# Attention into two mixture stages on one core: first-batch scores of two heads issued in turn on both row halves, second-batch sinks on all rows, new durations for the planner

## The chip, the cores and the metric

The kernel runs on one core of a Trainium2 chip. The metric is the device time of one execution in microseconds; lower is better. The time of the kernel before is the median of three runs.

## The reference

Sliding-window attention with sink positions, then two dense stages on its output (token-major, 1536 x 512), all in float32:

```
scores = q @ k.T / 8; keep = (key < n_sink) | (0 <= query - key < window)     # batch 2, 8 heads, 768, 64
a = exp(where(keep, scores, -1e9) - max); a = a / (sum(a) + 1e-9); x = a @ v   # n_sink 4, window 128
out1 = sum_e p[:, e] * (relu(x @ w1[e]) @ w2[e])     # 4 experts, 512 -> 1024 -> 512, p = normalised domain_probs
out  = ((out1 @ w_a) * (out1 @ w_b)) @ w_out         # 512 -> 1536 -> 512
```

## The kernel before, in words

Each float32 factor is split into a high and a low part, and a product is the sum of three TensorE products (high x high, high x low, low x high).

**Attention.** A unit is one batch b, one block m of 256 queries (3 per batch) and one pair of heads hp (4): 12 units per batch. `scores` makes, for each of the two heads h and two query tiles qi, a product of 128 queries by up to 288 keys (a previous block, 32 sink columns, the own block) into one PSUM bank; VectorE adds the penalty and takes the minimum as it reads the bank, ScalarE takes the exponential with its sum, and after the second tile of a head VectorE adds epsilon to both sums, takes reciprocals, and `nc.either` scales the weights on GpSimd, ScalarE or VectorE. `values` transposes the weights of the unit before, splits them (tile pt), multiplies them by the values (vv), and for m > 0 adds the sink part from sq, sk and the sink values vs.

The head size is 64, half of TensorE's 128 rows. In the first batch a head's queries and keys lie on its own 64 partitions (0 to 63 or 64 to 127), and a score product is three half-row matrix products, qh x kh, qh x kl, ql x kh (`factors`, first form); its sinks are two full-row products for both heads together. In the second batch high and low keys are stacked on all 128 partitions (two full-row products per score product), while the sink of one head is one half-row product on that head's 64 partitions, `vsink[own, hp, 0, :], sk[own]`. In the trace the score products are bank<-kk,qh and bank<-kk,ql, the sinks bank<-sk,vs, the weighted values bank<-pt,vv, transposes bank<-ident,...

**The stages.** First the 12 units of batch 0 run, with two plain experts for batch 0 (tiles xh, uh, dh) from the second block on; then the other experts of batch 0 by a seven-product scheme (tiles th, uh, dh) with the 12 units of batch 1 beside them; then batch 1's experts and the gated stage (tiles yt), with the conversion of the gate weights beside.

**Order.** The three parts between `nc.start()` and `nc.run()` are planned. Instructions are noted as nodes in program order; successive TensorE instructions into the same bank are one node (`note`). `cost` gives each a duration, `run` works out due times backward from TensorE's program order, and places nodes by readiness and due time on the engines V, S, G, T and the DMA queue D (SyncE's), TensorE at most 8 nodes ahead. Where a node has several ways (`either`, `copied`, `combined`), the plan chooses the engine. What runs on the chip is the resulting order for each engine, with semaphores. In the first part the score banks are two ("s" is (0, 1)), in the second one.

Every instruction recorded by the planner carries line 355 in the profile, the call in `run`; so tiles tell them apart.

Of the kernel before, what the change touches and what calls it, by code (L numbers as in the profile page):

```python
# [1 line left out]

# [16 lines left out]
P = 128  # L19
SC = 32  # L20
# [7 lines left out]
def f32(ap):  # L28
    return ap.bitcast(F32)
# [65 lines left out]
class Plan:  # L95
# [22 lines left out]
    def either(self, *ways):  # L118
# [4 lines left out]
        else:  # L123
            self.note(ways)

    def start(self):
        self.nodes, self.seen, self.at, self.key, self.last = [], {}, 0.0, None, None

    @staticmethod
# [18 lines left out]
    @staticmethod  # L148
    def cost(engine, name, args, kw):

        size = 1
        for d in kw.get("out", args[0] if args else None).shape[1:]:
            size *= d
        psum = any("PSUM" in str(getattr(v, "space", "")) for v in (*args[1:], *(v for k, v in kw.items() if k != "out")))
        if engine == "T":
            return 3 + size / 2.4 * (2 if name == "transpose" else 1)
        if engine == "V":
            fast = name in ("tensor_copy", "tensor_scalar") and not psum
            return 65 + size * (0.52 if fast else 1.04) + (55 if fast and hasattr(kw.get("scalar1"), "ap") else 0)
        if engine == "S":  # L160
            return (50 if psum else 95) + size / 1.2 + (180 if "accum_out" in kw else 0)
        return {"G": 150 + size * 2.1, "D": 60 + size * 1.42}[engine]

    @staticmethod
# [12 lines left out]
    def note(self, ways):  # L177
        engine, name, call, args, kw = ways[0]
        outs = [kw[k] for k in ("out", "accum_out") if kw.get(k) is not None]
        ins = [v for k, v in kw.items() if k not in ("out", "accum_out")]  # L180
        rest = list(args)
        if not outs:
            outs.append(rest.pop(0))
        ins = [v for v in ins + rest if hasattr(v, "ap") or hasattr(v, "tensor")]
        places = [self.region(v) for v in outs]
        node = None
        if engine == "T":
            key = places[0][0], self.turn.get(places[0][0])
            node = self.last if self.key == key else None
        if engine != "T" and self.key and any(self.region(v)[0] == self.key[0] for v in (*ins, *outs)):  # L190
            self.key = None
        if node is None:
            node = {"deps": set(), "n": len(self.nodes), "at": self.at, "ways": {w[0]: [0.0, [], False] for w in ways}}
            self.nodes.append(node)
            if engine == "T":
                self.key, self.last = key, node
        for e, name, call, args, kw in ways:
            way = node["ways"][e]
            way[0] += self.cost(e, name, args, kw)
            way[1].append((call, args, kw))  # L200
            way[2] = way[2] or self.shares(e, name, args, kw)
        node["e"], node["cost"] = engine, node["ways"][engine][0]
        if engine == "T":
            self.at = node["at"] + node["cost"]
        for v in ins:
            self.touch(node, self.region(v), False)
        for r in places:
            self.touch(node, r, True)
# [152 lines left out]
def tile_kernel(ctx, tc, a0, a1, vs, limit, places, dp, w1, w2, wa, wb, wo, out):  # L361
# [105 lines left out]
    def split(hi, lo, src, psum=False):  # L467
        copied(hi, src)
        if psum:
            nc.vector.tensor_tensor(out=lo, in0=src, in1=f32(hi), op=sub)  # L470
        else:
            combined(lo, src, f32(hi), sub)
# [103 lines left out]
    def sink_values(ab, b):  # L576

        raw = ab.tile([P, HP, D], F32, tag="tmp", name="vsr")
        nc.sync.dma_start(out=raw, in_=vs[b])
        if b:  # L580
            v = ab.tile([P, HP, 1, 2 * D], F32R, tag="vs", name="vs", bufs=1)
            held["vs", b] = v
            split(v[:, :, 0, 0:D], v[:, :, 0, D:], raw)
            return
        v = ab.tile([P, HP, 2, 2 * D], F32R, tag="vs", name="vs", bufs=1)
        held["vs", b] = v

        nc.gpsimd.memset(f32(v), 0.0)
        for h in range(2):
            r, c = slice(64 * h, 64 * h + 64), slice(64 * h, 64 * h + 64)  # L590
            nc.scalar.activation(out=v[r, :, 0, c], in_=raw[r], func=copy)
            r = slice(64 * h, 64 * h + 32)
            nc.vector.tensor_tensor(out=v[r, :, 1, c], in0=raw[r], in1=f32(v[r, :, 0, c]), op=sub)

    def scores(pools, raw, u):
# [20 lines left out]
        if b == 0:  # L616
# [6 lines left out]
            def factors(h, q, k):  # L623
                hs = slice(64 * h, 64 * h + 64)
                return [(x[hs, q], kk[hs, y, k]) for x, y in ((qh, 0), (qh, 1), (ql, 0))]
# [16 lines left out]
        st = ab.tile([P, 2, 4], F32, tag="st", name="st")  # L642
        sq = ab.tile([P, 2, 2, 2, SC], F32, tag="sq", name="sq") if m else None
        u.update(vv=vv, pp=pp, sq=sq)
        for h in range(2):
            for qi in range(2):
                c = 2 * h + qi
                k0 = qi * (P + SC)
                ks, use = (slice(k0, k0 + WIN), slice(0, WIN)) if m or qi else (slice(c0, c0 + 256), cur)
                sp = bank([P, ks.stop - ks.start], "s")  # L650
                parts = factors(h, slice(qi * P, (qi + 1) * P), ks)
                for n, (lhs, rhs) in enumerate(parts):
                    nc.tensor.matmul(out=sp, lhsT=lhs, rhs=rhs, start=n == 0, stop=n == len(parts) - 1)
                seen, least = pp[:, h, qi, use], low[:, slot, c:c + 1]
                nc.vector.tensor_tensor_reduce(
                    out=seen, in0=sp[:, 0:use.stop - use.start], in1=pen[:, min(2 * m + qi, 2), use],
                    scale=-1.0 / 8.0, scalar=3e38, op0=add, op1=ALU.min, accum_out=least,
                )
                nc.scalar.activation(
                    out=seen, in_=seen, func=ACTF.Exp, scale=-1.0, bias=least, accum_out=st[:, h, qi:qi + 1],  # L660
                )
                if c == 0:
                    combined(parts_[1], vr, f32(parts_[0]), sub)
                if qi == 0:
                    yield
            rs = st[:, h, 2:4]
            nc.vector.tensor_scalar(out=rs, in0=st[:, h, 0:2], scalar1=EPS, scalar2=None, op0=add)
            nc.vector.reciprocal(out=rs, in_=rs)
            if m:
                combined(  # L670
                    sq[:, :, h], pp[:, h, :, P:P + SC].unsqueeze(2).to_broadcast([P, 2, 2, SC]),
                    rs.unsqueeze(2).unsqueeze(3).to_broadcast([P, 2, 2, SC]), ALU.mult,
                )
            for q0, cols in ((0, slice(0, WIN)),) if m else ((0, cur), (1, prev)):
                seen, r = pp[:, h, q0:, cols], rs[:, q0:]
                n = seen.shape[1]
                nc.either(
                    ("gpsimd", "tensor_tensor", dict(
                        out=seen, in0=seen, in1=r.unsqueeze(2).to_broadcast(list(seen.shape)), op=ALU.mult
                    )),  # L680
                    *(("scalar", "activation", dict(
                        out=seen[:, i], in_=seen[:, i], func=copy, scale=r[:, i:i + 1]
                    )) for i in range(n)),
                    *(("vector", "tensor_scalar", dict(
                        out=seen[:, i], in0=seen[:, i], scalar1=r[:, i:i + 1], scalar2=None, op0=ALU.mult
                    )) for i in range(n)),
                )
            yield
        yield

    def values(pools, u, x):
# [31 lines left out]
        def weighted(h):  # L723
            own, oth = slice(64 * h, 64 * h + 64), slice(64 - 64 * h, 128 - 64 * h)
            sk = made.get("sk")
            if b == 0:

                if h == 0:
                    made["o"] = bank([P, 256], "o")
                op, mm = made["o"], []  # L730
                for j, s0 in blocks:
                    mm += [
                        (vv[:, j, 3 * a + h:3 * a + h + 2].rearrange("p a d -> p (a d)"), part(h, s0, o))
                        for a, o in ((0, 0), (0, 5), (1, 0))
                    ]
                if m > 0 and h:
                    mm += [(vsink[:, hp, a, :], sk) for a in range(2)]
                first, last = h == 0, h == 1
            else:

                op, mm = bank([P, 256], "o"), []
                for j, s0 in blocks:
                    mm += [(vv[:, j, 2 * h:2 * h + 2].rearrange("p a d -> p (a d)"), part(h, s0, o)) for o in (0, 5)]
                if m > 0:
                    mm.append((vsink[own, hp, 0, :], sk[own]))
                first = last = True
            for n, (lhs, rhs) in enumerate(mm):
                nc.tensor.matmul(
# [872 lines left out]
```

## Time and profile before

| | before |
|---|---|
| median of 3 runs (lowest, highest) | 952.56 us (951.9, 953.61) |
| profiled execution: its own time, its span | 951.72 us, 949.6 us |
| mean granted TensorE clock | 0.988 |
| busy share TensorE, VectorE, ScalarE, GpSimd | 97%, 78%, 43%, 34% |
| TensorE instructions | 4845 |
| HBM read, written | 131.10 MB, 83.36 MB |

The busy time of TensorE is that of overlapping instructions: a product's listed duration holds the way through the array, and the next starts before it ends. Starts tell how fast they follow each other. A share of a stage is read from a table of stretches, not from the whole span. Starts and stretches are given in us from the span's start.

### The profile page before, as it was taken

The page shows a single profiled execution, that of the slowest core. Times are in us where ns is not written, and L with a number is a line of the kernel's source. Part 1 is how long each engine was busy: PE and PEld are TensorE (multiplying, and loading weights), DVE is VectorE, ACT ScalarE, POOL GpSimd, SP SyncE. Part 2 cuts the span into 40 slices and gives each one's busy share as a digit, 9 for nine tenths or more (in the row PEclk, how much of TensorE's full clock was granted, in tenths as well). Part 3 has the DMA queues.
Part 4 walks back from the last instruction along what each step waited for, and adds up shares of the span by engine and source line. Part 5 has one row for each costly group of instructions (what it writes and reads, how often), then busy time and mean ns, then how long its engine had stood idle before and what let it go on. Part 6 is the DMA issues. An engine that isn't in the chain of part 4 may idle for free.

```text
span 949.6 us, 13937 instructions
## 1 busy us (share of the span) xinstructions
PE 920.8 (97%) x4845; PEld 824.8 (87%) x4845; DVE 741.1 (78%) x1516; ACT 404.3 (43%) x946; POOL 324.2 (34%) x328
## 2 busy tenths in 40 slices
PE   7999989999999999999999999999999999999996
PEld 6778878898888888888989989999887789999995
DVE  6798789999999998997876878799898985333343
ACT  6677557766656573521222312143453453211111
POOL 3565445646544651520200110044254543110100
PEclk9699999999999999999999999999999999999998
DMA  4250068886566744587867777877778878755552
GB/s 150 93 204 25 2 211 319 289 289 233 181 232 239 287 170 154 202 314 253 304 225 284 248 263 245 289 252 250 272 257 296 285 287 314 268 199 199 201 198 93
DMA packets 84752, 215.47 MB, mean 227 GB/s; under 512 B 7872, under 2 KB 42176, under 8 KB 84672
## 3 DMA queue, kind: packets, MB, share of 16 engines
q1 hardware_dynamic: 84672, 214.49, 64.6%
q8 instruction: 40, 0.66, 0.3%
q14 instruction: 40, 0.33, 0.1%
HBM read 131.10 MB, written 83.36 MB: 226 GB/s over the span
## 4 chain that ended last, share of the span: by engine, by line
PE 77%; DVE 13%; DMA 5%; ACT 2%; issue 2%; POOL 1%; SPq 1%; DVEq 0%; ACTq 0%; POOLq 0%
PE bank L355 77%; DVE tu L355 2%; DMA rawu<-gu 2%; DVE ul L355 2%; DVE y L355 1%; DVE kk L355 1%; DVE c L355 1%; DVE pp L355 1%; DVE sums L355 1%; DVE hl L355 1%; DMA rawu<-in_w 1%; DVE st L355 1%; DMA scr<-in_dp 1%; DMA araw<-in_a 1%; SPq L355 1%
## 5 line engine op out<-in xcount | busy, mean ns | idle before, releaser
L355 PE MATMUL bank<-dh,hh 128*128 128x512 f32 x528 | 210.2, 398 | 0.0
L355 PE MATMUL bank<-dl,hh 128*128 128x512 f32 x528 | 208.5, 395 | 0.0
L355 PE MATMUL bank<-dh,hl 128*128 128x512 f32 x528 | 208.0, 394 | 0.0
L355 PE MATMUL bank<-xh,uh 128*128 128x384 f32 (+1 forms) x384 | 129.7, 338 | 0.7 <-DVE r L355 0.7
L355 PE MATMUL bank<-xl,uh 128*128 128x384 f32 (+1 forms) x384 | 127.2, 331 | 0.0
L355 PE MATMUL bank<-xh,ul 128*128 128x384 f32 (+1 forms) x384 | 127.1, 331 | 0.0
L355 PEld LDWEIGHTS bank<-dl,hh 128*128 128x128 f32 x528 | 99.0, 187 | 21.7
L355 PE MATMUL bank<-th,uh 128*128 128x384 f32 x324 | 109.7, 339 | 3.9 <-DVE c L355 2.5
L355 PEld LDWEIGHTS bank<-dh,hh 128*128 128x128 f32 x528 | 99.2, 188 | 13.9 <-issue 0.3
L355 PEld LDWEIGHTS bank<-dh,hl 128*128 128x128 f32 x528 | 99.2, 188 | 12.6
L355 PE MATMUL bank<-tl,uh 128*128 128x384 f32 x324 | 109.2, 337 | 0.1
L355 PE MATMUL bank<-th,ul 128*128 128x384 f32 x324 | 108.8, 336 | 0.0
L355 ACT ACTIVATE r<-bank 128x384 f32<-128x384 f32 x73 | 35.8, 491 | 146.5 <-PE bank L355 145.9
L355 ACT ACTIVATE hh<-c 128x384 fp32r<-128x384 f32 x98 | 50.8, 519 | 96.7 <-DVE c L355 95.5
L355 DVE TENSOR_TENSOR c<-bank,r 128x384 f32<-128x384 f32 x108 | 59.8, 554 | 35.1 <-PE bank L355 34.5
L355 DVE SCALAR_TENSOR_TENSOR y<-bank,prob,y 128x512 f32<-128x512 f32 x108 | 80.0, 744 | 7.3 <-PE bank L355 6.6
L355 DVE TENSOR_TENSOR c<-bank,u 128x384 f32<-128x384 f32 x54 | 29.9, 553 | 67.6 <-PE bank L355 64.4
L355 PEld LDWEIGHTS bank<-xh,uh 128*128 128x128 f32 x384 | 72.7, 189 | 7.3 <-issue 1.1
L355 PEld LDWEIGHTS bank<-xl,uh 128*128 128x128 f32 x384 | 72.8, 190 | 4.4
L355 PEld LDWEIGHTS bank<-xh,ul 128*128 128x128 f32 x384 | 72.7, 189 | 0.0
L355 PEld LDWEIGHTS bank<-th,uh 128*128 128x128 f32 x324 | 60.8, 188 | 9.1 <-DVE c L355 3.7
L355 POOL TENSOR_TENSOR ul<-sums,uh 128x256 fp32r<-128x256 f32 (+1 forms) x39 | 40.6, 1043 | 80.7 <-ACT uh L355 80.6
(147 smaller groups left out, 1860.5 us busy)
## 6 DMA issues: line engine op xcount, KB each, us to landing
ue<-uh SPq DMA_DIRECT2D x14, 896.0 KB, 4.3
ue<-ul SPq DMA_DIRECT2D x14, 896.0 KB, 6.1
uh<-ue SPq DMA_DIRECT2D x14, 896.0 KB, 4.8
ul<-ue SPq DMA_DIRECT2D x14, 896.0 KB, 6.8
ug<-uh SPq DMA_DIRECT2D x12, 896.0 KB, 5.4
ug<-ul SPq DMA_DIRECT2D x12, 896.0 KB, 7.8
uh<-ug SPq DMA_DIRECT2D x12, 896.0 KB, 4.7
ul<-ug SPq DMA_DIRECT2D x12, 896.0 KB, 6.8
```

What stands on the lines that cost most here:

```text
L355: call(*args, **kw)
```

## The change

Four things change. In the first batch, `product` issues a query tile's products for both heads in turn (head 0, head 1, three times) into two banks, as one node of the plan, held together by `nc.together()`; both heads' sums and reciprocals are then one instruction each. In the second batch the sink values get a second, zero half, so that each head's sink is a product on all rows. The second batch's scores keep the order by heads. The planner's durations of TensorE instructions and of scaled copies on ScalarE change.

```diff
+    @contextmanager
+    def together(self):
+        self.hold, self.key = True, None
+        yield
+        self.hold, self.key = False, None
...
-            return 3 + size / 2.4 * (2 if name == "transpose" else 1)
+            half = "lhsT" in kw and kw["lhsT"].shape[0] < P
+            return 1 + size * (0.84 if name == "transpose" else 0.35 if half else 0.4535)
...
-            return (50 if psum else 95) + size / 1.2 + (180 if "accum_out" in kw else 0)
+            return (50 if psum else 95) + size / 1.2 + (180 if "accum_out" in kw else 0) + (
+                85 if hasattr(kw.get("scale"), "ap") else 0)
...
-            node = self.last if self.key == key else None
+            node = self.last if self.key == key or self.hold and self.key else None
...
-            v = ab.tile([P, HP, 1, 2 * D], F32R, tag="vs", name="vs", bufs=1)
+            v = ab.tile([P, HP, 2, 2 * D], F32R, tag="vs", name="vs", bufs=1)
             held["vs", b] = v
-            split(v[:, :, 0, 0:D], v[:, :, 0, D:], raw)
+            nc.gpsimd.memset(f32(v), 0.0)
+            for h in range(2):
+                r = slice(64 * h, 64 * h + 64)
+                split(v[r, :, h, 0:D], v[r, :, h, D:], raw[r])
...
+        def product(qi, heads):
+            k0 = qi * (P + SC)
+            ks, use = (slice(k0, k0 + WIN), slice(0, WIN)) if m or qi else (slice(c0, c0 + 256), cur)
+            sps = [bank([P, ks.stop - ks.start], "s") for _ in heads]
+            parts = [factors(h, slice(qi * P, (qi + 1) * P), ks) for h in heads]
+            with nc.together():
+                for n in range(len(parts[0])):
+                    for sp, some in zip(sps, parts):
+                        lhs, rhs = some[n]
+                        nc.tensor.matmul(out=sp, lhsT=lhs, rhs=rhs, start=n == 0, stop=n == len(some) - 1)
+            for h, sp in zip(heads, sps):
...
+        def normalised(heads):
+            h0, h1 = heads[0], heads[-1] + 1
+            nc.vector.tensor_scalar(
+                out=st[:, h0:h1, 2:4], in0=st[:, h0:h1, 0:2], scalar1=EPS, scalar2=None, op0=add
+            )
+            nc.vector.reciprocal(out=st[:, h0:h1, 2:4], in_=st[:, h0:h1, 2:4])
+            for h in heads:
...
+        if b == 0:
+            product(0, (0, 1))
+            lows()
+            yield
+            yield
+            product(1, (0, 1))
+            normalised((0, 1))
+            yield
+            yield
+        else:
+            for h in range(2):
+                product(0, (h,))
+                if h == 0:
+                    lows()
+                yield
+                product(1, (h,))
+                normalised((h,))
+                yield
...
-                    mm.append((vsink[own, hp, 0, :], sk[own]))
+                    mm.append((vsink[:, hp, h, :], sk))
```

Here `lows` is the same low part of the values as before, and the reading of a bank, the exponential and the scaling inside `product` and `normalised` are the lines of before.

## Rows read from the trace of the kernel before

**Rows 1.** Table of stretches: busy us and (x) instructions by engine, granted clock, DMA.
```profile
22.00:29.00 7.00, 6.35 (x38) 4.63 (x36) 5.83 (x21) 5.64 (x19) 5.20 (x6) 1.00 0.26 83
29.00:46.00 17.00, 17.00 (x66) 14.50 (x66) 10.75 (x40) 10.16 (x30) 7.42 (x8) 0.50 0.31 96
46.00:60.00 14.00, 13.55 (x96) 11.68 (x96) 13.88 (x37) 10.49 (x29) 8.23 (x7) 1.00 0.42 120
60.00:103.00 43.00, 42.18 (x277) 35.20 (x276) 35.98 (x112) 31.58 (x86) 24.43 (x30) 1.00 0.24 88
150.00:375.00 225.00, 222.83 (x1206) 198.39 (x1206) 211.57 (x442) 141.53 (x349) 121.33 (x124) 1.00 0.68 236
650.00:800.00 150.00, 142.70 (x734) 128.47 (x733) 131.15 (x212) 66.75 (x139) 71.02 (x59) 1.00 0.79 277
```

**Rows 2.** TensorE's waits by releaser, 0 to 104 us: total us, times, longest.
```profile
PE bank L355 <- DVE low L355: 1.8, 3, 1.3
```

**Rows 3.** TensorE's timeline from 76.8 us: start, duration, instruction.
```profile
76.84 0.53 PE L355 MATMUL bank<-kk,qh 64*128 64x288 f32 x2
...
77.43 1.32 PE L355 MATMUL bank<-pt,vv 128*128 128x256 f32 x9
78.67 0.53 PE L355 MATMUL bank<-kk,qh 64*128 64x288 f32 x2
```

**Rows 4.** The same from 81.9 us.
```profile
81.90 0.53 PE L355 MATMUL bank<-kk,qh 64*128 64x288 f32 x2
...
82.89 0.38 PE L355 MATMUL bank<-xh,uh 128*128 128x256 f32 x1
```

**Rows 5.** The same from 95.4 us.
```profile
95.41 0.54 PE L355 MATMUL bank<-kk,qh 64*128 64x288 f32 x4
...
96.01 0.85 PE L355 MATMUL bank<-pt,vv 128*128 128x256 f32 x5
```

**Rows 6.** The same from 30.6 us.
```profile
30.66 0.85 PE L355 MATMUL bank<-kk,qh 64*128 64x288 f32 x2
...
31.67 1.65 PE L355 MATMUL bank<-pt,vv 128*128 128x256 f32 x6
33.25 0.85 PE L355 MATMUL bank<-kk,qh 64*128 64x288 f32 x2
```

**Rows 7.** The same from 224.2 us, around one sink of the second batch.
```profile
224.29 0.64 PE L355 MATMUL bank<-pt,vv 128*128 128x256 f32 x4
224.86 0.38 PE L355 MATMUL bank<-sk,vs 64*128 64x256 f32 x1
225.17 0.50 PE L355 MATMUL bank<-dh,hh 128*128 128x512 f32 x1
225.50 0.40 PE L355 MATMUL bank<-dh,hl 128*128 128x512 f32 x1
225.74 0.40 PE L355 MATMUL bank<-dl,hh 128*128 128x512 f32 x1
```

**Rows 8.** Groups by form: 46 to 103, 29 to 46, 150 to 375 us; busy, mean ns.
```profile
L355 PE MATMUL bank<-kk,qh 64*128 64x288 f32 x51 | 12.7, 339 | 0.0
...
L355 PE MATMUL bank<-kk,qh 64*128 64x288 f32 x12 | 4.9, 505 | 0.0
...
L355 PE MATMUL bank<-sk,vs 64*128 64x256 f32 x16 | 6.1, 381 | 0.0
```

**Rows 9.** Groups by form of VectorE (0 to 104 us) and ScalarE (whole span).
```profile
L355 DVE CUSTOM_DVE_ANT_0 pp<-bank,pen 128x288 f32<-128x288 f32 x40 | 17.7, 450 | 5.6 <-PE bank L355 5.6
L355 DVE TENSOR_SCALAR st<-st 128x2 f32<-128x2 f32 x23 | 6.7, 297 | 1.6 <-POOL kk L355 1.1 <-ACT pp L355 0.5
L355 DVE RECIPROCAL st<-st 128x2 f32<-128x2 f32 x23 | 3.6, 161 | 0.2
...
L355 ACT ACTIVATE pp<-pp,st 128x288 f32<-128x288 f32 x46 | 22.1, 528 | 9.7 <-DVE sq L355 6.0 <-POOL sq L355 3.6
```

**Rows 10.** One tile's instructions (vs): durations min/median/max in ns.
```profile
L355 POOL MEMSET vs<- x1: 952/952/952, 2.8 to 2.8; 128x1024 f32 x1
```

More of the change, by code (lines that the diff above doesn't have):

```diff
@@ L1 @@
-from contextlib import ExitStack
+from contextlib import ExitStack, contextmanager
 import itertools
@@ L124, in either @@
             self.note(ways)
+    @contextmanager
[3 more added lines that the diff above has]
+        self.hold, self.key = False, None
     def start(self):
+        self.hold = False
         self.nodes, self.seen, self.at, self.key, self.last = [], {}, 0.0, None, None
@@ L644, in scores @@
         u.update(vv=vv, pp=pp, sq=sq)
-        for h in range(2):
-            for qi in range(2):
-                c = 2 * h + qi
[L648 to L653, printed above, removed]
+        def product(qi, heads):
[9 more added lines that the diff above has]
+            for h, sp in zip(heads, sps):
+                c = 2 * h + qi
                 seen, least = pp[:, h, qi, use], low[:, slot, c:c + 1]
@@ L661, in scores @@
                 )
[L662 to L687, printed above, removed]
@@ L688, in scores @@
-            yield
+        def normalised(heads):
[5 more added lines that the diff above has]
+            for h in heads:
+                rs = st[:, h, 2:4]
+                if m:
+                    combined(
+                        sq[:, :, h], pp[:, h, :, P:P + SC].unsqueeze(2).to_broadcast([P, 2, 2, SC]),
+                        rs.unsqueeze(2).unsqueeze(3).to_broadcast([P, 2, 2, SC]), ALU.mult,
+                    )
+                for q0, cols in ((0, slice(0, WIN)),) if m else ((0, cur), (1, prev)):
+                    seen, r = pp[:, h, q0:, cols], rs[:, q0:]
+                    n = seen.shape[1]
+                    nc.either(
+                        ("gpsimd", "tensor_tensor", dict(
+                            out=seen, in0=seen, in1=r.unsqueeze(2).to_broadcast(list(seen.shape)), op=ALU.mult
+                        )),
+                        *(("scalar", "activation", dict(
+                            out=seen[:, i], in_=seen[:, i], func=copy, scale=r[:, i:i + 1]
+                        )) for i in range(n)),
+                        *(("vector", "tensor_scalar", dict(
+                            out=seen[:, i], in0=seen[:, i], scalar1=r[:, i:i + 1], scalar2=None, op0=ALU.mult
+                        )) for i in range(n)),
+                    )
@@ new lines, in scores @@
+        lows = lambda: combined(parts_[1], vr, f32(parts_[0]), sub)
+        if b == 0:
+            product(0, (0, 1))
+            lows()
+            yield
+            yield
[12 more added lines that the diff above has]
+                yield
```

## The prediction

> **What bounds the kernel now.** I read the table of stretches first [rows 1]. Its columns are the busy time of each engine; the reader is to see that TensorE is never idle for long: 42.2 of 43 us between 60 and 103 us, 222.8 of 225 between 150 and 375, and that VectorE is the second limit: 13.9 of 14 us at 46 to 60, 84% at 60 to 103, 94% at 150 to 375. The list of TensorE's waits [rows 2] says the same from the other side: up to 104 us it waited 1.8 us in all for VectorE's reading of the scores. So time taken out of TensorE's instruction stream should shorten the span, as far as VectorE follows.
>
> "Busy" hides a loss, so I read TensorE's timeline by its start times. With full rows a 128x256 product starts 0.118 us after the one before (four from 224.29 to 224.86, less 0.10 for what follows) [rows 7]. A stretch of three half-row score products runs from 76.84 to 77.43, 0.59 us [rows 3]; six in a row take 0.99 [rows 4], so one product costs 0.13 and a stretch has 0.19 over that. The nine full-row products behind it take 1.24 us to 78.67 where 9 x 0.118 = 1.06 are due: 0.18 more, one part for the change of rows before them, one for that after. A stretch on half rows thus costs 0.19 + 0.19 = 0.38 us beyond its products. The sink of the second batch, one half-row product alone, shows this again: 0.31 where 0.12 is due, 0.10 ahead of it, and 0.33 instead of 0.24 behind: 0.19 + 0.10 + 0.09 = 0.38 us [rows 7].
>
> And once the order happened to bring the two heads' products in turn, on alternating halves: six from 95.41 to 96.01, 0.60 us instead of 0.99 [rows 5]. Less the 0.19, that is 0.41 for six, 0.13 for two: the halves ran side by side. This is what the change makes of all of the first batch's scores.
>
> **The change part by part.** *Scores at full clock, 46 to 103 us.* 51 products with qh there make 25.5 groups of three [rows 8], in 21 stretches: 17 with three, 3 with six on one half after the other, 1 in turns. With both ends' cost: 17 x (0.59 + 0.19) + 3 x (0.99 + 0.19) + (0.60 + 0.19) = 13.3 + 3.5 + 0.8 = 17.6 us. After, 12.75 pairs at 0.79: 10.1 us. That takes 7.5 us from TensorE. Of 46 to 60 us, with five of these stretches (5 x 0.78 - 2.5 x 0.79 = 1.9 us), VectorE is full and I count half, 1.0. Of the other 5.6 I count 4.7: VectorE's 36.0 us of work in 43 would then be 94% of 38.3, but it is relieved too, as below.
>
> *Scores at the low clock, 29 to 46 us.* The granted clock is 0.50 there, TensorE's level of 1.2 GHz [rows 1]. A stretch of three takes 1.01 us, and the six products behind it 1.58 [rows 6]. These cost about 0.21 each as 256 / 1.2 GHz, so 0.30 is the ends'. Six groups of three [rows 8] stand in four stretches of three and one of six: 4 x 1.31 + (1.01 + 0.75 + 0.30) = 7.3 us. Pairs at this clock don't stand in the trace; if halves run side by side as above, 1.01 + 0.30 = 1.31 each, 3.9 for three. Saved 3.4, counted 2.5, because VectorE (10.75 of 17) follows until it is full from 46 us on.
>
> *Scores before 29 us.* 48 - 25.5 - 6 = 16.5 groups, eight pairs; at 0.75 us each (2.06 - 1.31) 6.0 us is the upper end. But TensorE waits there for chains, and a wait is added: a pair needs both score banks empty, where a product needed one. Behind it the whole TensorE queue stands. The next pair of a unit waits for two readings of 0.45 us [rows 9], 0.9 us and the way there and back. Later than 29 us a unit has about 9 us (57 us for 6.4 units), and other products stand between its pairs; early it has about 6 (25 us for 4.1 units), and the 1.8 us of waiting for VectorE [rows 2] could double. So -1.8 to +6.0; I take +1, near the rows that show waiting.
>
> *The sinks.* 16 half-row products [rows 8] become full-row ones and lose 16 x 0.38 = 6.1 us. VectorE is at 94% there: 211.6 us of work in 225 [rows 1] would be 97% of 219. Bounds 0 and 6.1; I take half, 3.1. Clearing the new zeros is one fill like that of 0.95 us on GpSimd in the first batch [rows 10], and one split becomes two; the first use is units later, so it is hidden; uncovered it would be about 2 us. The load of these values is the same DMA.
>
> *Sums and reciprocals for both heads at once.* 12 fewer additions at 0.30 and 12 fewer reciprocals at 0.16 on VectorE [rows 9]: 5.5 us less work at 0 to 103 us. It is off TensorE's path, so no term of its own; it is why I let most of the score saving through. Head 0's normalisation now waits for head 1's exponentials too; its transposes come only with the next unit's scores, some 9 us later, so I put that at 0.
>
> *The scheduler's durations.* They change no instruction but its place and, for optional work, its engine, in every stage; the DMA and GpSimd queues are ordered anew too. By the cost lines a 512-column product was planned at 3 + 512 / 2.4 = 216 ns and is now at 1 + 512 x 0.4535 = 233; the row has 0.24 from 225.50 to the next [rows 7]. So the plan before ran TensorE some 7% fast. A scaled copy of 288 columns on ScalarE was planned at 95 + 240 = 335 and is now at 420 ns; the row has 528 [rows 9], so some may go to VectorE where it is full. What there is to win is TensorE's waiting at 650 to 800 us: 142.7 busy of 150, 7.3 us [rows 1]. What there is to lose has no row; I bound it by the same size. I take 0, with -7 to +7.
>
> One rule speaks against the score terms. A pair takes 0.13 us by the row above [rows 5], nearly twice the rate. By the Trainium skill (TensorE: Matmul & The Clock Gate, Part 3: Packing small matmuls) four row tiles gained 3.07 times, 77% of four; an estimate from that page, 77% for two halves, would make six products 0.52 instead of 0.41 and the saving 1.7 us smaller. The row is of this very operation, so I keep it.
>
> **Sum.** 1.0 + 4.7 + 2.5 + 1 + 3.1 + 0 = 12.3 us off the profiled execution's 951.72 (span 949.6): 939.4. The three runs' median lies 0.84 above it: 940.
>
> **The rivals.** *VectorE takes over (0.20).* For: it is full at 46 to 60 us and 94% at 150 to 375. Against: TensorE waited for it hardly at all, and it gets 5.5 us back. Then the sinks and 46 to 60 us give 0, the rest half: 2.8 + 1.7 + 0 = 4.5, so 948; in a quarter of this case nothing.
>
> *The clock stays low longer (0.08; slower).* It was granted in full at 22 to 29 us, when TensorE was busy 6.35 of 7 us, and fell to 0.50 at 29 [rows 1]. Pairs make the early stream thinner still, so the rise may come later, or a fall come back. At the low clock a product takes 0.21 instead of 0.118, 0.8 us more for each us of work. Low from 22 to 60 us costs 0.8 x 13 + 3 = 13.4, the whole gain: that is the point from which it decides; low to 74 us, 0.8 x 25 + 3 = 23 (13 and 12 us of work after the saving, 3 for 22 to 29), so about 963. By the Trainium skill (TensorE: Matmul & The Clock Gate, Part 1: The HAM clock gate) the throttled state is the default and activity releases it; no row here shows how pairs count for that. Against: from 46 us on the stream is dense and gets denser.
>
> *The pairs don't run side by side (0.04).* Then 12.75 x (0.99 + 0.19) = 15.0 against 17.6, 2.6 us, and three sixes at 2.06 against 7.3, 1.1; with the sinks 6 to 7 us: 946. The row at 95.41 speaks against it.
>
> *The new plan decides (0.18).* Better by 7 us in the last stages (0.10): 933. Worse by 7 or more (0.08): 947 and up, about a quarter of it slower than before.
>
> **How the numbers follow.** The forecast, 934 to 946, has 0.50. To hold 8 in 10 the range takes in the better plan with more from the early pairs (930) and VectorE's case up to no gain (953); the clock's case lies outside. A measurement can tell 0.2%, 1.9 us. Faster: 0.50 + 0.15 + 0.04 + 0.10 + 0.03 = 0.82. Within: 0.05 + 0.03 = 0.08. Slower: 0.08 + 0.02 = 0.10.
>
> **What would show it.** In the timeline after, score stretches of six at about 0.60 us; 24 stretches or fewer; no half-row sink, and 0.24 behind each. The last score product ends some 9 us ahead of 103 us. TensorE's waits for the readings of scores stay under 4 us. VectorE's busy share at 150 to 375 rises to 96% without TensorE waiting over 5 us. The forecast is wrong if the stretch of granted clock 0.50 reaches past 60 us, if VectorE's waits on TensorE's list grow by over 6 us, or if 650 to 800 us holds over 14 us of idle TensorE.

## The result, and the profile after

The changed kernel takes 943.09 us (median of 4 runs, 942.14 to 945.87) beside 953.09 us for the kernel before on the same chips: a ratio of 0.990 (0.9875 to 0.9931), 9 to 10 us faster. The forecast was 940 us, 930 to 953.

The table of stretches of the changed kernel at the times of [rows 1] (its profiled execution took 945.87 us, span 944.1; that of before 951.72):

```profile
29.00:46.00 17.00, 13.49 (x95) 11.45 (x96) 16.09 (x43) 12.62 (x37) 12.01 (x11) 0.90 0.35 114
60.00:103.00 43.00, 41.90 (x315) 37.13 (x316) 39.53 (x109) 22.23 (x65) 20.39 (x25) 1.00 0.09 27
150.00:375.00 225.00, 218.03 (x1185) 194.28 (x1184) 213.85 (x448) 134.22 (x323) 109.22 (x110) 0.99 0.64 228
650.00:800.00 150.00, 145.15 (x745) 131.40 (x744) 127.61 (x205) 65.59 (x139) 72.48 (x63) 0.99 0.81 284
```

From 29 to 46 us the granted clock is 0.90 where it was 0.50, and TensorE is idle for 3.5 us where it never was; at 150 to 375 it is idle for 7.0 instead of 2.2. What TensorE waited for, up to 104 us (first line) and at 150 to 375 us (the longest three; all of its waits there, 6.9 us, were ended by VectorE):

```profile
PE bank L365 <- DVE low L365: 4.8, 4, 2.3
...
PE bank L365 <- DVE r L365: 3.7, 3, 1.9
PE bank L365 <- DVE low L365: 1.1, 2, 0.8
PE bank L365 <- DVE y L365: 1.0, 2, 0.8
```

Its timeline at a pair and at a sink, to be held beside [rows 4], [rows 5] and [rows 7]:

```profile
71.62 0.53 PE L365 MATMUL bank<-kk,qh 64*128 64x288 f32 x4
72.00 0.29 PE L365 MATMUL bank<-kk,ql 64*128 64x288 f32 x2
72.22 0.66 PE L365 MATMUL bank<-ident,pp 128*128 128x128 f32 x4
...
237.41 0.28 PE L365 MATMUL bank<-sk,vs 128*128 128x256 f32 x1
237.53 0.40 PE L365 MATMUL bank<-dh,hh 128*128 128x512 f32 x1
237.76 0.40 PE L365 MATMUL bank<-dh,hl 128*128 128x512 f32 x1
```

Six score products take 0.60 us, a sink 0.12 and the product behind it 0.23: both edits do to TensorE what was said. Where the time went is read best between places that both programs pass: the products of 384 columns come 42 to an item in the same order (2268 of them, 54 items), so their starts mark the stages. Up to the first (item 0) is the first stage, 124.8 us before and 112.0 after. Items 3 to 12 are the second batch's attention, items 13 to 21 what follows it. The same table at these marks, kernel before and then changed kernel:

```profile
0.00:124.80 124.80, 116.34 (x672) 99.26 (x673) 94.85 (x303) 79.49 (x223) 62.60 (x87) 0.93 0.33 106
173.50:355.80 182.30, 180.13 (x977) 160.24 (x976) 173.83 (x367) 119.02 (x291) 102.69 (x105) 1.00 0.68 238
374.80:501.40 126.60, 126.60 (x638) 113.76 (x638) 107.86 (x192) 37.60 (x72) 27.79 (x23) 1.00 0.74 259
```

```profile
0.00:112.00 112.00, 96.89 (x673) 83.44 (x674) 98.72 (x297) 72.86 (x211) 58.49 (x82) 0.98 0.38 120
160.50:346.70 186.20, 179.31 (x977) 159.46 (x976) 177.48 (x379) 113.95 (x277) 93.67 (x95) 0.99 0.64 234
365.20:496.80 131.60, 128.92 (x639) 113.08 (x638) 111.93 (x203) 36.52 (x69) 26.30 (x19) 1.00 0.72 248
```

The first stage gained 12.8 us, more than the 9.2 forecast. The second batch's attention lost 3.9 although its sinks had become cheaper, and the stretch behind it lost 5.0. In both VectorE has 11 or 12 instructions more, ScalarE and GpSimd fewer. (In this execution the clock was also at half from 227.7 to 231.1 us, inside the second batch's attention; 3.4 us at half can take 1.7 us from TensorE, which is not the whole loss.) So a right total hides a gain that is larger than forecast and a loss that was put at zero.

### The profile page after: what moved, and what is told of

Same layout as the page of the kernel before. It is cut to its first block, busy times and chain, and to the rows that moved or that the text cites. A ratio compares the mean times of both kernels' runs of the same rounds, so it can differ in the third digit from the quotient of the medians.

```text
span 944.1 us, 13891 instructions
## 1 busy us (share of the span) xinstructions
PE 904.0 (96%) x4845; PEld 808.4 (86%) x4845; DVE 757.6 (80%) x1543; ACT 384.2 (41%) x905; POOL 315.4 (33%) x321
## 4 chain that ended last, share of the span: by engine, by line
PE 46%; DVE 31%; DMA 14%; issue 4%; POOL 3%; ACT 2%; SPq 0%; DVEq 0%; POOLq 0%; ACTq 0%
PE bank L365 46%; DVE tu L365 6%; DMA gu<-tu 4%; DVE y L365 3%; DMA rawu<-in_w 3%; DMA rawu<-gu 3%; DVE c L365 2%; DVE hl L365 2%; DVE pp L365 2%; DVE sums L365 2%; DVE ul L365 2%; DVE kk L365 2%; DVE x L365 1%; DVE pt L365 1%; POOL sums L365 1%
## 5 line engine op out<-in xcount | busy, mean ns | idle before, releaser
L365 PEld LDWEIGHTS bank<-dl,hh 128*128 128x128 f32 x528 | 99.4, 188 | 21.7
L365 POOL TENSOR_TENSOR tu<-tu 128x512 f32<-128x512 f32 x15 | 19.9, 1324 | 175.9 <-DVE tu L365 175.9
```

Of the source, the lines that this page charges most:

```text
L365: call(*args, **kw)
```

## The experiments

Ratios are to the kernel before on the same chip, with 95% intervals.

**Each part by itself.** `e1` keeps the two edits of the sinks alone, `e2` the scores and sums, `e3` the durations, `e4` scores and sinks:

```diff
# e4: the changed kernel with
-            return 1 + size * (0.84 if name == "transpose" else 0.35 if half else 0.4535)
+            return 3 + size / 2.4 * (2 if name == "transpose" else 1)
...
-            return (50 if psum else 95) + size / 1.2 + (180 if "accum_out" in kw else 0) + (
-                85 if hasattr(kw.get("scale"), "ap") else 0)
+            return (50 if psum else 95) + size / 1.2 + (180 if "accum_out" in kw else 0)
# e2: e4 with the sinks as before
-                    mm.append((vsink[:, hp, h, :], sk))
+                    mm.append((vsink[own, hp, 0, :], sk[own]))
...
# e1: the kernel before with the second batch's vs tile and this line as in the change; e3: with the durations alone
```

> The kernel before with the second batch's sinks on all rows alone. By the prediction's step each of the 16 sinks gives back 0.38 us of TensorE (6.1 us), and VectorE lets half of it through: 3 us faster (1 to 6). Rival, VectorE is the bound at 150 to 375 us: no change within 1 us. Either way a sink's start to the next is 0.12 us instead of 0.31.

948.56 us, ratio 0.9949 (0.992 to 0.9978): 4.9 us faster (2.1 to 7.6), as expected. It looks as if VectorE let most of the 6.1 through, but the interval holds the half that was counted as well.

> The kernel before with the first batch's scores in pairs and the shared sums and reciprocals alone, durations of the planner as before. Theory: the pairs made the changed kernel's first stage 12.8 us shorter, whatever the durations, and that reaches the end: 9 us faster (7 to 13). Rival, the durations made half of that first stage's gain: 4 to 6 us faster.

937.94 us, 0.9812 (0.9781 to 0.9843): 18 us faster, twice what was expected. The first stage ends at 110.4 us instead of 124.8. Of the 18, some 4 us go with the granted clock (an estimate, below under the clock).

> The kernel before with the planner's new durations alone (half-row products, which stand singly here, are planned at 0.35 ns per column too). Theory: the second stage of the changed kernel lost 8 to 10 us of what the first had gained, with the sinks' 6 us on top, and the new plan is the cause: 3 to 8 us slower than before. Rival, the durations are neutral or help and the loss comes from VectorE having no room for an earlier TensorE: 0 to 4 us faster.

958.78 us, 1.006 (1.0033 to 1.0087): 5.7 us slower, as expected; at the same granted clock it is about 10 (an estimate, below under the clock).

> Pairs and sinks together, durations of the planner as before. Theory (the new durations cost the second stage): 13 us faster than before (10 to 16), and the stretch from the first 384-column product to the seventeenth item 290 us or less. Rival (VectorE has no room there): 7 to 10 us faster as the changed kernel, the second stage as long as in that.

933.03 us, 0.9772 (0.9743 to 0.9802): 21.7 us faster by the ratio, 10 us faster than the changed kernel. Its second batch's attention takes 178.5 us:

```profile
0.00:109.50 109.50, 96.80 (x673) 83.66 (x674) 91.06 (x287) 73.75 (x215) 62.51 (x87) 0.98 0.38 122
160.70:339.20 178.50, 175.09 (x976) 158.35 (x975) 172.85 (x363) 118.76 (x285) 104.73 (x105) 1.00 0.68 240
357.60:485.10 127.50, 126.89 (x639) 113.57 (x638) 108.56 (x193) 37.42 (x72) 28.13 (x23) 1.00 0.74 257
```

The rival, that VectorE had no room for an earlier TensorE, falls. The theory had the direction and missed both of its numbers: 21.7 is more than 10 to 16, and from the first 384-column product to the seventeenth item it is 296 us, not 290 or less (297 in the kernel before, 304 in the changed kernel). The parts add up without the durations (4.9 + 17.9 = 22.8 for 21.7); these cost 10 us.

**What the durations do.** `e6` has TensorE's new durations alone, `e7` the scaled copies' alone, `e12` both with one more constant:

```diff
# e12: the changed kernel with
-            return 65 + size * (0.52 if fast else 1.04) + (55 if fast and hasattr(kw.get("scalar1"), "ap") else 0)
+            return 110 + size * (0.52 if fast else 1.04) + (55 if fast and hasattr(kw.get("scalar1"), "ap") else 0)
```

> The changed kernel with the new durations of TensorE alone (scaled copies on ScalarE planned as before). Theory: these later due times move work between VectorE and GpSimd in the second stage and are most of the 10 us that the durations cost: 940 to 944. Rival, the scaled copies' longer duration moves work to VectorE and is the cause: 932 to 936.

934.79 us, 0.9816 (0.9773 to 0.986).

> The changed kernel with the longer duration of scaled copies on ScalarE alone (TensorE planned as before). Theory (TensorE's durations are the cause): 932 to 937. Rival (the scaled copies' are): 939 to 944, with some 13 more multiplications on VectorE in the first stage.

931.22 us, 0.9782 (0.974 to 0.9824).

Neither alone is the cause. On `e6` the theory missed; the time lies in its rival's range, but the rival's cause, the scaled copies' duration, is refuted by `e7`, which came out at 931 where that cause asked for 939 to 944. The stretch of items 3 to 12 of `e3`, `e6` and `e7`, and for `e6` that of items 13 to 21:

```profile
173.70:359.90 186.20, 181.63 (x976) 160.10 (x974) 177.84 (x370) 115.92 (x279) 104.11 (x107) 1.00 0.67 238
```

```profile
156.90:334.80 177.90, 175.54 (x976) 158.10 (x976) 169.10 (x371) 117.33 (x286) 101.14 (x103) 1.00 0.71 253
353.20:485.20 132.00, 128.91 (x638) 113.06 (x638) 112.05 (x203) 36.28 (x69) 25.77 (x19) 1.00 0.71 246
```

```profile
159.60:335.90 176.30, 174.50 (x976) 158.67 (x975) 170.58 (x364) 118.17 (x285) 98.06 (x100) 1.00 0.68 243
```

Two effects are to be seen. At items 13 to 21 TensorE's durations alone suffice: VectorE gets 203 instructions instead of 192, and the stretch takes 132 us instead of 127, in `e6` as in the changed kernel (203, 131.6). At items 3 to 12 only both together do harm: ScalarE has 277 to 279 instructions instead of 285 to 291, VectorE is busy for 177 to 178 us instead of 169 to 174, and the stretch follows: 186 us with 177 to 178, 176 to 182 with less. VectorE's idle time in it is 5 to 9 us in every one of these kernels, and `e3` and the changed kernel take the same 186.2 us although the sinks are cheaper for TensorE in the second. That points to VectorE's work as what sets the length there. At items 13 to 21 VectorE is not full (112 of 132 us); TensorE's waits there were for single late results of VectorE, 2.6 us of its 2.7 idle ones in the changed kernel.

> The changed kernel with both new durations, and every instruction of VectorE planned 45 ns longer (65 to 110 ns of fixed cost), so that the plan gives VectorE fewer of the optional operations. Theory: the 10 us that both durations cost are work put on VectorE, which has under 9 us of idle time in the 180 us of the second batch's attention: its instructions between items 3 and 12 fall from 378 to 366 or fewer, that stretch from 186 us to 180 or less, the whole to 933 to 939. Rival: it is the order that the two durations give together, not VectorE's share: 941 or slower.

937.31 us, 0.9823 (0.9788 to 0.9857): 6 us of the 10 came back with both durations still new, as the theory had it.

```profile
0.00:113.20 113.20, 95.46 (x672) 82.17 (x673) 95.10 (x276) 78.01 (x224) 65.85 (x90) 1.00 0.37 116
162.60:338.10 175.50, 174.21 (x977) 158.61 (x976) 170.18 (x360) 120.46 (x291) 97.67 (x101) 1.00 0.69 247
356.40:484.40 128.00, 127.01 (x640) 113.55 (x639) 106.19 (x191) 40.27 (x77) 24.16 (x21) 1.00 0.73 256
```

VectorE has 360 instructions instead of 379 and the stretch 175.5 us instead of 186.2; at items 13 to 21 it has 191 and 128.0. What did not come back lies in the first stage, 113.2 us here and 109.5 in `e4`. So from item 3 on the price of the durations goes with the work that the plan puts on VectorE. The new constant also changes the order, so that VectorE's share alone does it is likely and not shown. Why the plan does so at items 3 to 12 only when both durations change stays open.

**What the pairs give.** In `e5` a pair's products come head after head, in `e9` a stretch of six holds both query tiles of one head; `e8`, the base of `e9`, is `e4` with sums and reciprocals by head (in `e9` head 0's come before head 1's products):

```diff
# e5: e4 with
-                for n in range(len(parts[0])):
-                    for sp, some in zip(sps, parts):
-                        lhs, rhs = some[n]
-                        nc.tensor.matmul(out=sp, lhsT=lhs, rhs=rhs, start=n == 0, stop=n == len(some) - 1)
+                for sp, some in zip(sps, parts):
+                    for n, (lhs, rhs) in enumerate(some):
+                        nc.tensor.matmul(out=sp, lhsT=lhs, rhs=rhs, start=n == 0, stop=n == len(some) - 1)
# e8: e4 with
-            normalised((0, 1))
+            for h in range(2):
+                normalised((h,))
# e9: e8 with product() taking (head, query tile) pairs, three products after three
-            product(0, (0, 1))
...
-            product(1, (0, 1))
+            product([(0, 0), (0, 1)])
...
+            product([(1, 0), (1, 1)])
```

> Pairs and sinks with the durations of before, but within a pair the three products of head 0 come first, then the three of head 1: same plan, same number of row changes, nothing side by side. Theory: halves running side by side are worth 0.39 us a pair at full clock, 24 pairs: 9 us slower than pairs and sinks (933 to 942; 6 to 11). Rival: the pairs' gain is that of fewer row changes and of the shared sums, TensorE's streaming is hidden: 0 to 3 us slower.

933.1 us, 0.9799 (0.9757 to 0.984): as `e4` within the intervals. The reason is in TensorE's timeline of `e5`:

```profile
69.22 0.54 PE L363 MATMUL bank<-kk,qh 64*128 64x288 f32 x4
69.59 0.30 PE L363 MATMUL bank<-kk,ql 64*128 64x288 f32 x2
69.82 0.62 PE L363 MATMUL bank<-pt,vv 128*128 128x256 f32 x3
```

The program issues qh, qh, ql of head 0 and then of head 1; the trace has four products with qh before the first with ql, and 0.60 us for six. TensorE ran the second head's products beside the first's of its own accord. This experiment took nothing away, so it decided nothing about the worth of running side by side.

> Pairs and sinks with the durations of before, but the sums and reciprocals are made for each head by itself as in the kernel before: 12 more additions and 12 more reciprocals on VectorE. Theory (the prediction's): that is off TensorE's path, 0 to 2 us slower than pairs and sinks. Rival: VectorE is the other limit of the first stage, and its 5 us are why pairs gave 18 us and not 9: 4 us slower or more.

932.84 us, 0.9799 (0.9757 to 0.984): no loss. The shared sums are worth nothing that can be measured.

> As sums by head (pairs and sinks, durations of before, sums made by head), but a node of six score products now holds both query tiles of one head instead of both heads of one tile: as few row changes, the same halves one after the other, so nothing can run side by side. The run with heads in line did not tell this: its trace shows the second head's products starting 10 ns after the first's although they were issued three later. Theory: side by side is worth 0.99 - 0.60 = 0.39 us for each of 24 stretches: 6 to 10 us slower than sums by head (932.84), so 939 to 943. Rival: fewer row changes were the whole gain, 0 to 3 us slower.

943.18 us, 0.9902 (0.9869 to 0.9936), 10 us slower than `e8`. Two tiles on the same half did not overlap, 0.98 us for six:

```profile
73.45 0.53 PE L363 MATMUL bank<-kk,qh 64*128 64x288 f32 x2
73.82 0.29 PE L363 MATMUL bank<-kk,ql 64*128 64x288 f32 x1
73.94 0.43 PE L363 MATMUL bank<-kk,qh 64*128 64x288 f32 x2
74.22 0.29 PE L363 MATMUL bank<-kk,ql 64*128 64x288 f32 x1
74.43 0.55 PE L363 MATMUL bank<-ident,pp 128*128 128x128 f32 x3
```

The first stage tells it without the later ones, `e8` and then `e9`:

```profile
0.00:106.90 106.90, 96.40 (x672) 82.55 (x673) 92.66 (x309) 75.49 (x219) 62.60 (x85) 1.00 0.38 124
```

```profile
0.00:116.40 116.40, 105.74 (x672) 91.72 (x673) 93.89 (x299) 79.79 (x226) 63.12 (x87) 1.00 0.35 113
```

9.5 us, where 24 x 0.39 = 9.4 were expected. That it agrees to 0.1 us is luck: some of the 24 ran before the clock's first rise, where a pair costs more, or beside waits. The other 8.4 us to the 124.8 of before are what is left of the change when nothing overlaps: 22 stretches on half rows instead of 33, which is 11 x 0.38 = 4.2 us, and with them whatever the other plan and the clock give, some 4 us.

**The clock.** Before its first rise, at about 20 us, the profile has no record of the clock and the tables show 1.00. The products there take what they take at half: two with qh 0.84 us, as 0.85 in [rows 6], against 0.53 in [rows 3]. From the kernel before:

```profile
4.31 0.84 PE L355 MATMUL bank<-kk,qh 64*128 64x288 f32 x2 [4.31 <-ACT qh L355]
```

In `e10` (on `e4`) and `e11` (on the kernel before) seven products of 512 columns on a constant tile run while the first load is under way:

```diff
+        busy = const.tile([P, 512], mybir.dt.bfloat16, name="busy")
+        tc.nc.vector.memset(busy, 0.5)
+        for _ in range(7):
+            tc.nc.tensor.matmul(out=ps[7], lhsT=busy[:, 0:P], rhs=busy, start=True, stop=True)
```

> Pairs and sinks with the durations of before, and seven products of zeros' place (a constant bf16 tile, 512 columns each, into a bank used later, never read) that keep TensorE busy while the first load is under way. Same plan. Theory: with pairs the clock was granted from 20 us on with one fall of 3.4 us; granted earlier it finds TensorE waiting for VectorE and ScalarE: 0 to 2 us faster than pairs and sinks. Rival: the low clock of the first 20 us holds the start up: 4 us or more faster.

935.83 us, 0.9817 (0.9783 to 0.9851): no gain over `e4`. The clock rose at 4.3 us, fell at 7.7 and came back at 21.4. So most of the first 20 us stayed at half, and the rival, that this holds the start up, was hardly tested.

> The kernel before with the same seven products at the start. Theory: the surplus of the pairs over the prediction's 9 us in the first stage (15 were measured) is the clock, which stood at half for 17 us from 29 us on in the kernel before and for 3.4 us with pairs; where these products move the fall, 2 to 6 us faster than before; where the granted clock stays as it was, no change. Rival: the surplus is TensorE's time that VectorE let through, the clock is worth under 1 us even where it changes.

957.31 us, 1.0047 (1.0021 to 1.0073): slower, against both. In the first stage the clock was at half for 10 us in two falls instead of 17 in one:

```profile
30.00:36.70 6.70, 6.70 (x26) 5.36 (x24) 4.88 (x19) 3.57 (x12) 3.47 (x4) 0.50 0.51 161
36.70:53.80 17.10, 15.75 (x110) 13.41 (x108) 16.49 (x44) 14.31 (x40) 10.48 (x9) 1.00 0.28 77
53.80:57.20 3.40, 3.08 (x14) 2.86 (x14) 2.75 (x9) 1.73 (x5) 1.06 (x2) 0.50 0.95 325
```

and that stage ended at 124.0 us instead of 124.8, although the first score product came 0.24 us later. At 36.7 to 53.8 us TensorE has the full clock and idles for 1.4 us, VectorE is busy for 96%: the clock gave back what VectorE then took. So 7 us less at half were worth about 1 us in this stage. What the clock adds there to the gain of the pairs, which had at most 3.4 us at half after the first rise, stays open between that and the 4 us left over in `e9`, which had no fall before item 0.

For the whole kernel the clock is worth more than that. The kernel before ran 64 times beside the experiments, and its time goes with the execution's mean granted clock: the 18 executions at 0.994 or more have a median of 949.1 us, the 11 under 0.986 one of 956.8. A line through all 64 gives 6.4 us less for 0.01 more. Their mean is 0.990 (0.989 on the chip of `e1` to `e4`); `e1` has 0.990, `e2` 0.995, `e3` and `e4` 0.996, `e11` 0.983, the changed kernel 0.995. That line gives four estimates. Next to nothing of the sinks' 4.9 us is the clock's. Of the 18 us in `e2` and the 21.7 in `e4`, some 4 are. The durations cost 10 us in `e3`, as they do in the changed kernel, and not 5.7. And the lower clock of `e11` makes up its whole loss; in its profiled execution the clock was at half again at 135.7 to 139.1, 692.1 to 698.9 and 733.0 to 736.5 us. Why the mean clock is higher with the pairs and with the durations, and lower behind seven products at the start, was not settled.

## Why the prediction was right or wrong

The time and its sign were right, but that the total came out so near is luck: the gains were larger than counted, in part by a clock that fell less, for which no term stood, and the durations, counted at 0, took 10 us of them back.

*Scores, 46 to 103, 29 to 46 us and before.* The mechanism was right; the size that I let through was not. TensorE's own saving was worked out as 7.5 + 3.4 + 6.0 = 16.9 us, of which I counted 9.2 because VectorE was nearly full. With the durations left out the first stage gained 14.4 (`e2`) and 15.3 us (`e4`), part of which may be the clock's. VectorE hardly held TensorE up at a busy share over 90%; in `e4`, from 60 us to its last score product, TensorE is never idle, and in the 25 us behind that VectorE has room again:

```profile
60.00:84.40 24.40, 24.40 (x197) 21.59 (x197) 22.78 (x75) 17.87 (x51) 12.59 (x17) 1.00 0.14 45
84.40:109.50 25.10, 24.85 (x165) 22.45 (x165) 18.40 (x43) 8.11 (x21) 10.43 (x16) 1.00 0.25 84
```

VectorE's work up to item 0 is 91.1 us in `e4` where it was 94.9. I had taken its share of a stretch of 14 us [rows 1] for a limit of the stage. The wait for two empty banks showed, as 4.8 us of waiting for the reading of scores in the changed kernel where [rows 2] has 1.8. That is beyond the 4 us I had set, and the stage gained all the same. The 7.0 us of idle TensorE at 150 to 375 us are beyond my sign of 5, too.

*Rows 5 read wrongly.* The six products at 95.41 us were not issued in turn; a score product was one node there, so they came three after three. The number was right, the cause was half right: neighbours on different halves run side by side in either order (`e5`).

*The sinks.* I counted 3.1 us, and 4.9 (2.1 to 7.6) were measured in `e1`. In place the second batch's attention shrank by 4.1 us from `e2` to `e4`. The fill and the second split were put at nothing, or 2 us uncovered; between items 1 and 3, where they stand, the stretch grew by 2.6 us. `e2` between items 1 and 3 and between 3 and 12, then `e4` between 1 and 3:

```profile
122.60:159.10 36.50, 36.50 (x202) 33.31 (x201) 35.46 (x84) 27.52 (x75) 19.41 (x20) 1.00 0.86 292
159.10:341.70 182.60, 180.24 (x976) 160.18 (x975) 174.68 (x367) 118.72 (x288) 102.60 (x104) 1.00 0.67 238
...
121.60:160.70 39.10, 37.45 (x203) 33.41 (x202) 37.00 (x83) 28.10 (x75) 23.40 (x27) 1.00 0.83 284
```

So they, or the other order that comes with them, were not hidden: the two stretches together give 1.5. The profiled execution of `e4` ends 4.5 us ahead of that of `e2` because it also won 1.0 up to item 1 and 2.0 behind item 12, which no row here puts down to the sinks.

*Sums and reciprocals.* They are worth nothing that can be measured, as said (`e8`).

*The scheduler's durations* are the step that failed: 0 counted, 7 either way as the bound; they cost 5.7 us alone (about 10 at the same granted clock) and 10 in the changed kernel, where the plan put 11 or 12 more instructions on VectorE in each of two stretches and both got longer. The sentence that scaled copies may go "to VectorE where it is full" named the mechanism and then gave it no price. That the plan ran TensorE 7% fast was true and no reason to hope: the durations are closer to the trace and the plan is worse.

*Rivals.* VectorE did take over, but where the durations gave it more work. The clock went the other way: up to item 0 it was at half for 3.4 us after the first rise instead of 17.1. Over the whole kernel some 3 us of the gain go with its mean, 0.995 instead of 0.990, as estimated above; a gain by the clock was not among the rivals. The two halves do run side by side: 0.60 us for six beside 0.98 in `e9`, both with 0.19 for the change of rows, is 0.41 to 0.79, a factor of 1.9. The prediction's estimate from the Trainium skill (TensorE: Matmul & The Clock Gate, Part 3: Packing small matmuls), 77% of two and so 0.52 us, had the saving smaller; these traces do not bear that out.

## What to carry to other kernels

Price a change of a planner's costs as a change of its own, by counting what moves to the engine that is nearly full, and run it apart from the edits it comes with: the kernel without it, 933.03 us (with the scaled copies' duration alone 931.22, the same within the intervals), beats both kernels here. Look at the clock of every execution before a difference of a few us is put down to an edit. Put half-row products of different halves next to each other and keep single ones out of full-row streams; a lone one cost 0.38 us beyond its streaming. And ask of a full engine whether its work can wait, before a saving beside it is halved.

## What the runs showed of the hardware

TensorE ran three products on one half of its rows beside three on the other although they were issued one group after the other, with starts about 10 ns apart in the trace of `e5`. A change between half and full rows cost 0.19 us each way here. Two products of the same half did not overlap: six took 0.98 us in `e9`, beside 0.60. A granted clock at half for 10 us instead of 17 shortened the first stage of `e11` by 0.8 us only, where VectorE was busy for 96% behind it; over whole executions of the kernel before 0.01 of mean granted clock went with 6.4 us.
